# Four of six tiles of y transposed by VectorE blocks and DMAs in place of TensorE

## The chip, the cores and the metric

The kernel runs on one core of a Trainium2 chip. The metric is the device time of one execution in microseconds. Before the change it is 945.48 us (median of 3 runs, 944.89 to 948.21).

## The reference, cut to what matters

Four batches of 448 tokens go through sigmoid attention (12 heads of 64), a gated two-layer stage and a token and channel mixer, all in float32.

```
x  = concat over heads of sigmoid(q k^T / 8 - log 448) v            # [448, 768]
xk = mu_k * x + (1 - mu_k) * x_prev ;  xr likewise                  # x_prev: the token before
y  = sigmoid(xr @ w_r) * (relu(xk @ w_k) ** 2 @ w_v)                # [448, 768]
h  = relu(y^T @ w_tok1) @ w_tok2                                    # mixes tokens: 448 -> 256 -> 448
u  = y + h^T
out = u + relu(u @ w_ch1) @ w_ch2                                   # mixes channels: 768 -> 1536 -> 768
```

## The kernel before

Activations lie with channels on the 128 partitions and tokens along the free axis, one batch at a time, in six tiles of 128 channels by 448 tokens. Every float32 operand of a product is carried as `hi + lo`, hi being the rounded operand and lo the remainder, and a product is three matmuls (hi·hi, hi·lo, lo·hi; lines 395, 397 and 398). `split` (lines 95 to 100) makes the pair: a copy on ScalarE or VectorE, then a subtraction on VectorE.

`first_part` computes one batch up to u. Its loop over six tiles at line 453 makes y: 24 matmuls per tile m against two chunks of w_v, then on line 459 VectorE multiplies the sum in PSUM into `rows[m]`. The token mixing that follows contracts over tokens, so it needs y with tokens on the partitions. `y_transpose(m)` (lines 442 to 451) does that on TensorE: four transposes of up to 128 by 128 into one PSUM buffer (line 448), then two splits out of PSUM into the tiles `yt` (tag A2), one for the first 384 tokens and one for the last 64, whose hi and lo share a chunk. It is called for tile m-1 in the middle of the product of tile m (line 458), and for the last tile after the first product of the token mixing (line 474). The token mixing (line 464) works on two halves of the channels: half 0 reads tiles 0 to 2 of `yt` in each of its matmuls, half 1 tiles 3 to 5.

Weights come as float64. On first use a chunk is loaded into a tile `raw` (pool `wraw`, two buffers), made float32 by `narrow` and stored to DRAM; later it is read back into `wd` (line 315, two buffers). `w_tick` (line 340) keeps this going: a split into `whi` and `wlo` (three buffers), then the next loads. All DMAs are issued by SyncE. The attention of the next batch is handed out between the products of the current one.

The order on each engine is made by the framework from tiles and dependences; the buffers of one tag are given out in the order of the code, while an instruction whose operands and buffer are there may stand ahead of code that comes before it.

Of the kernel before, what the change touches and what calls it, by code (L numbers as in the profile page):

```python
# [9 lines left out]
F32 = mybir.dt.float32  # L10
F32R = mybir.dt.float32r
U32 = mybir.dt.uint32
# [19 lines left out]
def f32(ap):  # L32
    return ap.bitcast(F32)
# [9 lines left out]
EARLY = 20  # L43
TOK2 = 20


# Heads (batch, head) whose second product runs in plain float32: more for TensorE, less for the
# engines that split operands.
NATIVE = {(0, 1), (0, 7), (0, 4), (1, 1), (0, 3), (1, 8), (1, 4), (0, 6), (0, 2), (0, 5), (1, 9), (0, 11)}


# [5 lines left out]
def kernel(  # L57
# [13 lines left out]
    w_ch2: bass.AP,  # L71
    out: bass.AP,
):
    # Activations lie channels by tokens, one batch at a time; lay_out() and kernel() make
    # and undo the layouts of the inputs and of the output.
    # Every float32 operand of a matrix product is carried as hi + lo, both float32r, where
    # hi is the rounded operand and lo the exact remainder.
    nc = tc.nc
    PE, ACT, DVE, POOL, SP = nc.tensor, nc.scalar, nc.vector, nc.gpsimd, nc.sync

# [14 lines left out]
    def split(hi, lo, src, engine):  # L95
        if engine is ACT:
            ACT.copy(hi, src)  # L97
        else:
            DVE.tensor_copy(hi, src)
        DVE.tensor_tensor(out=lo, in0=src, in1=f32(hi), op=ALU.subtract)  # L100

    # ---------------------------------------------------------------- attention
    # Keys and values of a head: three chunks of 128 tokens, and the last 64 tokens twice, so
    # that hi and lo of what multiplies them share one contraction.
    kns, qns, vns = {}, {}, {}

    def load_k(g):
# [11 lines left out]
            vns[g] = a2.tile([P, 2, 4, D], F32, tag="vn", name="vn")  # L119
            SP.dma_start(out=vns[g], in_=v[g])  # L120

    # The table that holds every function in use is loaded while the first inputs come.
    warm = const.tile([P, 1], F32, tag="warm", name="warm")
    DVE.memset(warm, 0.0)
    ACT.activation(warm, warm, AF.Sigmoid)
    # TensorE comes up to its clock on zeros meanwhile.
    zero = const.tile([P, S], BF16, tag="zero", name="zero")
    POOL.memset(zero, 0.0)
    idle = ps_av.tile([P, 512], F32, tag="av", name="idle")
# [20 lines left out]
        DVE.tensor_scalar(out=om, in0=m, scalar1=-1.0, scalar2=1.0, op0=ALU.mult, op1=ALU.add)  # L150
        mus[name] = (m, om)

    # x of one batch from column 1 on; column 0 is what precedes the first token.
    xe = big.tile([P, NT, 1 + S], F32, tag="xe", name="xe")
    POOL.memset(xe[:, :, 0:1], 0.0)

# [81 lines left out]
        DVE.tensor_tensor(out=xe[me, pr, 1:], in0=ps[me, :S], in1=tmp[me], op=ALU.add)  # L238

    def attention_units(b, then=()):  # L240
        # then: for each pair of heads what follows its part of x
        u = [lambda: unit_k(b, 0, 0), lambda: unit_q(b, 0, 0), lambda: unit_k(b, 0, 1)]
        for pr in range(NPAIR):
            nx = pr + 1 < NPAIR
            u.append(lambda pr=pr: unit_qk(b, pr, 0, 0))
            u.append(lambda pr=pr: unit_q(b, pr, 1))
            if pr:
                u.append(lambda pr=pr: unit_av(b, pr - 1, 1))
                u += [f[pr - 1] for f in then]
            u.append(lambda pr=pr: unit_qk(b, pr, 0, 1))  # L250
            if nx:
                u.append(lambda pr=pr: unit_k(b, pr + 1, 0))
            u.append(lambda pr=pr: unit_qk(b, pr, 1, 0))
            u.append(lambda pr=pr: unit_av(b, pr, 0))
            if nx:
                u.append(lambda pr=pr: unit_q(b, pr + 1, 0))
                u.append(lambda pr=pr: unit_k(b, pr + 1, 1))
            u.append(lambda pr=pr: unit_qk(b, pr, 1, 1))
        u.append(lambda: unit_av(b, NPAIR - 1, 1))
        u += [f[NPAIR - 1] for f in then]  # L260
        return u

    # ---------------------------------------------------------------- weights
    # They come in float64. Each chunk is made float32 when it is first used, kept so in
    # DRAM, and read from there afterwards.
    def narrow(dst, raw):
        # dst, uint32 words: the float32 of the float64 whose two words lie in raw.
        # The scale takes the exponent's bias from float64's to float32's; of the low word
        # the top three bits are left, rounded so that they stay three.
        lo, hi = raw[..., 0], raw[..., 1]  # L270
        ACT.activation(f32(dst), f32(hi), AF.Copy, scale=2.0**-112)
        if ENG("low", 0) is ACT:
            ACT.activation(lo, lo, AF.Copy, bias=0.4375, scale=0.875 * 2.0**-29)
        else:
            DVE.tensor_scalar(out=lo, in0=lo, scalar1=0.875 * 2.0**-29, scalar2=0.4375, op0=ALU.mult, op1=ALU.add)
        DVE.scalar_tensor_tensor(  # L276
            out=dst, in0=dst, scalar=3, in1=lo, op0=ALU.logical_shift_left, op1=ALU.bitwise_or
        )
        DVE.scalar_tensor_tensor(  # L279
            out=dst, in0=hi, scalar=0x80000000, in1=dst, op0=ALU.bitwise_and, op1=ALU.bitwise_or  # L280
        )
# [73 lines left out]
        wst["due"] = i  # L355
        return splits.pop(i)

    # w_tok2 stays on chip.
    wt2h = const.tile([P, 2, S], F32R, tag="wt2h", name="wt2h")
    wt2l = const.tile([P, 2, S], F32R, tag="wt2l", name="wt2l")  # L360

# [5 lines left out]
            narrow(d.bitcast(U32), raw)  # L367
            split(wt2h[:, j], wt2l[:, j], d, DVE)

    # ---------------------------------------------------------------- mixing  # L370
    def pair_tiles(tag, n):
        return tuple(big.tile([P, n], F32R, tag=tag + s, name=tag + s) for s in "hl")

# [13 lines left out]
        )  # L387
        split(col(dst[0], t), col(dst[1], t), t2, ENG("mix", b))

    # ---------------------------------------------------------------- moe and mixer  # L390
    def products(ps, n, count, parts, stacked=None):
        # parts yields per contraction tile: stationary hi, lo, moving hi, lo;
        # of the tile `stacked` the moving hi holds both.
        for i, (wh, wl, xh, xl) in enumerate(parts):
            PE.matmul(ps[:, :n], wh, xh, start=(i == 0), stop=False)  # L395
            if i != stacked:
                PE.matmul(ps[:, :n], wh, xl, start=False, stop=False)  # L397
            PE.matmul(ps[:, :n], wl, xh, start=False, stop=(i == count - 1))  # L398
            if i % 2 == 1 or i == count - 1:
                yield (3 if i % 2 == 0 else 6) * (n / 2.4 + 2.5)  # L400
                w_tick()
# [12 lines left out]
    def first_part(b, xr, xk, rows, u):  # L414
        rows[:] = [big.tile([P, S], F32, tag="r%d" % m, name="r%d" % m) for m in range(NT)]

        # r = sigmoid(xr @ w_r)
        for m in range(NT):
            ps = new_mm()
            yield from products(ps, S, NT, chunked(1, NT, xr))  # L420
            ACT.activation(rows[m], ps[:, :S], AF.Sigmoid)

        # kk = relu(xk @ w_k) ** 2
        kk = pair_tiles("M", 12 * S)
        for m in range(F // P):
            ps = new_mm()
# [7 lines left out]
                DVE.tensor_tensor(out=t2, in0=t1, in1=t1, op=ALU.mult)  # L434
            split(col(kk[0], m), col(kk[1], m), t2, ENG("kk", b))

        # y = r * (kk @ w_v); its transpose feeds the token mixing
        # (tokens in chunks of 128; of the last 64, hi and lo share a chunk).
        yt = pair_tiles("A2", 4 * C)
        ytv = [t.rearrange("p (r c) -> p r c", r=4) for t in yt]  # L440

        def y_transpose(m):
            ps = new_mm()
            psv = ps.rearrange("p (r c) -> p r c", r=4)
            ms = slice(m * P, (m + 1) * P)
            for r in range(4):
                n = P if r < 3 else TAIL
                PE.transpose(psv[:n, r], rows[m][:, r * P : r * P + n], ident)  # L448
            hi, lo = (t[:, :, ms] for t in ytv)
            split(hi[:, :3], lo[:, :3], psv[:, :3], ACT)  # L450
            split(hi[:TAIL, 3], hi[TAIL:, 3], psv[:TAIL, 3], ACT)

        for m in range(NT):
            ps = new_mm()
            for i, cost in enumerate(products(ps, S, 8, chunked(2, 4, kk))):
                yield cost
                if i == 1 and m:
                    y_transpose(m - 1)
            DVE.tensor_tensor(out=rows[m], in0=rows[m], in1=ps[:, :S], op=ALU.mult)

        # token mixing
        h1v = [t[:, : 2 * C].rearrange("p (j c) -> p j c", j=2) for t in pair_tiles("M", 12 * S)]
        wt1 = []
        for half in range(2):
# [35 lines left out]
                split(col(u[0][0], m), col(u[0][1], m), t1, ACT)  # L500
                split(col(u[1][0], m), col(u[1][1], m), rows[m], ACT)

    # Channel mixing takes two batches at a time, and the hidden channels in two halves.
    # Of the earlier batch, the sum waits in DRAM.
    away = [dram.tile([P, S], F32, tag="u%d" % m, name="u%d" % m) for m in range(NT)]
    part = [dram.tile([P, S], F32, tag="p%d" % m, name="p%d" % m) for m in range(NT)]

# [26 lines left out]
                    elif i == 0:  # L534
                        SP.dma_start(out=part[m], in_=z)

    # ---------------------------------------------------------------- schedule
    def mix_units(name, box, b):
        def mix(t):
            if t == 0:  # L540
# [12 lines left out]
            w_ready(1)  # L553
    w_ready(2)

    # Attention and mixing of later batches go between the products of earlier ones.
    t_a = 432 * PASS + 44 * (HC / 2.4 + 2.5)
    t_c = 864 * PASS

# [34 lines left out]


def lay_out(x):
    """The inputs in the order in which the chip reads them; each value stays as it is."""
    import numpy as np

    def chunks(w, parts=1):  # L600
        # [K, N] -> per 128 columns and part of K: partition, tile of K, column
        kt = w.shape[0] // (P * parts)
        w = w.reshape(parts, kt, P, w.shape[1] // P, P).transpose(3, 0, 2, 1, 4)
        return w.reshape(-1, P, kt * P)
# [18 lines left out]
        "moe2_w_ch2": chunks(x["moe2_w_ch2"], 2),  # L623
    }
    y = {n: np.ascontiguousarray(a) for n, a in y.items()}
    # The chip has no float64: those arrays go as the 64-bit words that they are.
    return {n: a.view(np.int64) if a.dtype == np.float64 else a for n, a in y.items()}


# [39 lines left out]
```

## Time and profile before

| | us |
|---|---|
| median of 3 runs | 945.48 |
| profiled execution, first to last instruction | 939.8 |
| TensorE busy | 929.6 |
| VectorE busy | 658.3 |
| ScalarE busy | 517.4 |

The profile is one execution. Its span leaves out what lies before the first and after the last instruction, 5.7 us against the median. A busy TensorE is not one at its peak, as matmuls overlap; the chain of waits and the distance between starts tell what one costs. Idle time of an engine that isn't the bottleneck costs nothing.

### The profile page before, as it was taken

To read this page: it belongs to the slowest core of one execution; us is meant where nothing else is said; L and a number is where in the kernel's file an instruction comes from. 1 tells how busy PE (TensorE), PEld (TensorE's weight loads), DVE (VectorE), ACT (ScalarE), POOL (GpSimd) and SP (SyncE) were. 2 spreads that over 40 slices of the span, in tenths; PEclk is the share of its full clock that TensorE was granted. 3 is DMA by queue.
4 is the path that set the end of the run, shared out by engine and by line. 5 is a ranking of instruction groups with operands and counts; after the bars stand their busy time and mean duration, and the time that the engine had idled before them with its cause. 6 is when DMAs were issued, how large, how long until landed. Compare 5 with 4: busy or idle time off the path is not lost.

```text
span 939.8 us, 12086 instructions
## 1 busy us (share of the span) xinstructions
PE 929.6 (99%) x4472; PEld 816.0 (87%) x4472; DVE 658.3 (70%) x1087; ACT 517.4 (55%) x794; POOL 1.2 (0%) x8
## 2 busy tenths in 40 slices
PE   8999999999999999999999999999999999999998
PEld 4476778788999999999999999999999999999997
DVE  8999999988557997778779479988744463332231
ACT  6998988774664857546641367767444342112210
POOL 0000000000000000000000000000000000000000
PEclk9999999999999999999999999999999999999999
DMA  7636675674343466554535333323334331332131
GB/s 239 220 135 233 246 243 190 226 237 145 117 127 111 141 217 229 190 201 172 185 130 181 122 114 108 110 68 104 107 96 129 107 110 51 94 122 70 51 112 59
DMA packets 57082, 137.37 MB, mean 146 GB/s; under 512 B 6592, under 2 KB 23488, under 8 KB 57024
## 3 DMA queue, kind: packets, MB, share of 16 engines
q1 hardware_dynamic: 57024, 136.61, 43.6%
q8 instruction: 35, 0.57, 0.2%
q14 instruction: 23, 0.19, 0.1%
HBM read 106.96 MB, written 29.62 MB: 145 GB/s over the span
## 4 chain that ended last, share of the span: by engine, by line
PE 87%; DVE 7%; ACT 4%; DMA 2%; issue 1%; ACTq 0%; DVEq 0%
PE psmm L398 25%; PE psmm L395 25%; PE psmm L397 24%; PE psc L195 3%; PE psc L196 3%; PE pav L233 2%; PE pav L228 2%; PE pav L235 2%; PE psmm L448 1%; ACT a L202 1%; DVE wlo L100 1%; DVE wd L276 1%; DMA raw<-in_moe_w_k_dram 1%; DVE wd L279 1%; DMA raw<-in_moe_w_r_dram 1%
## 5 line engine op out<-in xcount | busy, mean ns | idle before, releaser
L97 ACT CAST whi<-wd 128x768 fp32r<-128x768 f32 (+1 forms) x160 | 121.4, 759 | 237.7 <-PE psmm L397 217.2
L100 DVE TENSOR_TENSOR wlo<-wd,whi 128x768 fp32r<-128x768 f32 (+1 forms) x160 | 137.6, 861 | 101.4 <-ACT whi L97 100.0
L395 PE MATMUL psmm<-Mh,whi 128*128 128x448 f32 x480 | 177.2, 369 | 0.1
L398 PE MATMUL psmm<-Mh,wlo 128*128 128x448 f32 x480 | 176.2, 367 | 0.1
L397 PE MATMUL psmm<-Ml,whi 128*128 128x448 f32 x480 | 175.5, 366 | 0.0
L395 PE MATMUL psmm<-A2h,whi 128*128 128x448 f32 (+1 forms) x400 | 145.2, 363 | 1.1 <-ACT whi L97 1.1
L398 PE MATMUL psmm<-A2h,wlo 128*128 128x448 f32 (+1 forms) x400 | 144.9, 362 | 0.8 <-DVE wlo L100 0.8
L397 PE MATMUL psmm<-A2l,whi 128*128 128x448 f32 (+1 forms) x384 | 139.2, 363 | 0.0
L397 PE MATMUL psmm<-A1l,whi 128*128 128x448 f32 x288 | 105.5, 366 | 0.1
L398 PE MATMUL psmm<-A1h,wlo 128*128 128x448 f32 x288 | 105.4, 366 | 0.0
L395 PE MATMUL psmm<-A1h,whi 128*128 128x448 f32 x288 | 105.2, 367 | 0.0
L202 ACT ACTIVATE a<-psc 128x896 f32<-128x896 f32 x96 | 86.9, 913 | 30.7 <-PE psc L196 30.2
L398 PEld LDWEIGHTS psmm<-Mh,wlo 128*128 128x128 f32 x480 | 90.2, 188 | 10.5 <-DVE wlo L100 1.6
L395 PEld LDWEIGHTS psmm<-Mh,whi 128*128 128x128 f32 x480 | 90.2, 188 | 9.0 <-issue 0.7
L397 PEld LDWEIGHTS psmm<-Ml,whi 128*128 128x128 f32 x480 | 90.2, 188 | 7.0
L395 PEld LDWEIGHTS psmm<-A2h,whi 128*128 128x128 f32 x400 | 75.1, 188 | 8.6 <-ACT whi L97 1.7
L398 PEld LDWEIGHTS psmm<-A2h,wlo 128*128 128x128 f32 x400 | 75.1, 188 | 8.1 <-DVE wlo L100 1.9
L397 PEld LDWEIGHTS psmm<-A2l,whi 128*128 128x128 f32 x384 | 72.1, 188 | 5.9 <-DVE A2l L100 0.3
L195 PE MATMUL psc<-Q,KK 128*128 128x448 f32 x192 | 71.6, 374 | 0.5 <-ACT a L202 0.4
L196 PE MATMUL psc<-Q,KK 128*128 128x448 f32 x192 | 70.3, 367 | 0.7 <-DVE Q L100 0.7
L209 ACT CAST ah<-a 128x896 fp32r<-128x896 f32 x72 | 67.7, 943 | 1.1
L395 PEld LDWEIGHTS psmm<-A1h,whi 128*128 128x128 f32 x288 | 54.0, 188 | 6.8 <-issue 1.4
(87 smaller groups left out, 1329.3 us busy)
## 6 DMA issues: line engine op xcount, KB each, us to landing
wd<-w SPq DMA_DIRECT2D x66, 384.0 KB, 3.0
raw<-in_moe_w_ch_dram SPq DMA_DIRECT2D x24, 768.0 KB, 4.6
w<-wd SPq DMA_DIRECT2D x38, 384.0 KB, 2.6
qn<-in_q_dram SPq DMA_DIRECT2D x48, 224.0 KB, 2.8
wd<-w SPq DMA_DIRECT2D x42, 256.0 KB, 2.6
kn<-in_k_dram SPq DMA_DIRECT2D x24, 256.0 KB, 2.7
vn<-in_v_dram SPq DMA_DIRECT2D x24, 256.0 KB, 3.1
raw<-in_moe_w_k_dram SPq DMA_DIRECT2D x8, 768.0 KB, 5.0
```

The costliest lines, as they stand in the source:

```text
L97: ACT.copy(hi, src)
L100: DVE.tensor_tensor(out=lo, in0=src, in1=f32(hi), op=ALU.subtract)
L195: PE.matmul(ps[:, j, :S], K[:, c * P : (c + 1) * P], Q1, start=True, stop=False)
L196: PE.matmul(ps[:, j, :S], K[:, c * P : (c + 1) * P], Q2, start=False, stop=True)
L202: ACT.activation(a, ps[:, :, :S], AF.Sigmoid, bias=-math.log(S), scale=1.0 / math.sqrt(D))
L209: ACT.copy(ah, a)
L228: PE.matmul(ps[:D, :S], vs[:n, c], st[c // 2][:n, c % 2], start=(c == 0), stop=(c == 3))
L233: PE.matmul(ps[:, :S], vs[:, c], ah[:, c % 2], start=(c == 0), stop=(c == 3))
L235: PE.matmul(ps[:, :S], vs[:, c], al[:, c % 2], start=False, stop=False)
L395: PE.matmul(ps[:, :n], wh, xh, start=(i == 0), stop=False)
L397: PE.matmul(ps[:, :n], wh, xl, start=False, stop=False)
L398: PE.matmul(ps[:, :n], wl, xh, start=False, stop=(i == count - 1))
```

## The change

For batches 1 to 3, tiles 0 to 3 of y are no longer transposed on TensorE. `y_turn(m)` lets VectorE transpose `rows[m]` in blocks of 32 by 32 into a tile `turn`, which two neighbouring tiles share and which takes a buffer of the pool `wraw`. After the second tile of a pair, 16 DMAs (4 positions of the block among the tokens, 4 among the channels) carry its blocks to their tokens' partitions, into columns of the tiles of kk that nothing else uses (`spare`). Each moves 32 partitions by 4 (or 3) runs of 256 bytes. They are issued on SyncE four at a time after each step of the product. `y_split(m)` then splits `spare` into `yt` with the same two splits as before, in the products of tiles 4 and 5. Tiles 4 and 5, and all of batch 0, go as before. The other lines of the diff take out comments and write out a helper.

```diff
+TURNED = 4
+TURN = 1
+BLK = 32
...
+        turned = TURNED if b >= TURN else 0
+        spare = [f32(t[:, 8 * S : 8 * S + 8 * P]).rearrange("p (r s c) -> p r s c", r=4, s=4) for t in kk]
+        turn, carry = {}, []
+
+        def y_turn(m):
+            if m % 2 == 0:
+                t = wraw.tile([P, NT, P, 2], U32, tag="raw", name="turn").rearrange("p t n e -> p (t n e)")
+                turn[m // 2] = f32(t[:, : 2 * S]).rearrange("p (g c) -> p g c", g=S // BLK)
+            tv = turn[m // 2]
+            at = m % 2 * BLK
+            DVE.transpose(tv[:, :, at : at + BLK], rows[m].rearrange("p (g c) -> p g c", c=BLK))
+            if m % 2:
+                for d in range(4):
+                    for s in range(4):
+                        to = spare[m // 2][d * BLK : (d + 1) * BLK, : 4 if d < 2 else 3, s]
+                        carry.append((to, tv[s * BLK : (s + 1) * BLK, d::4]))
+
+        def y_split(m):
+            ms = slice(m * P, (m + 1) * P)
+            at = m % 2 * BLK
+            src = spare[m // 2][:, :, :, at : at + BLK]
...
+            hi, lo = (t[:, :, ms] for t in ytv)
+            split(blocks(hi[:, :3]), blocks(lo[:, :3]), src[:, :3], ACT)
+            split(blocks(hi[:TAIL, 3:]), blocks(hi[TAIL:, 3:]), src[:TAIL, 3:], ACT)
+
         for m in range(NT):
             ps = new_mm()
             for i, cost in enumerate(products(ps, S, 8, chunked(2, 4, kk))):
                 yield cost
                 if i == 1 and m:
-                    y_transpose(m - 1)
+                    (y_turn if m - 1 < turned else y_transpose)(m - 1)
+                for to, src in carry[:4]:
+                    SP.dma_start(out=to, in_=src)
+                del carry[:4]
+                if m >= 4 and i in (2, 3) and 2 * (m - 4) + i - 2 < turned:
+                    y_split(2 * (m - 4) + i - 2)
             DVE.tensor_tensor(out=rows[m], in0=rows[m], in1=ps[:, :S], op=ALU.mult)
```

## Rows read from the trace of the kernel before

**Rows 1.** The page: span, and each engine's busy us, share and instructions.
```profile
span 939.8 us, 12086 instructions
...
PE 929.6 (99%) x4472; PEld 816.0 (87%) x4472; DVE 658.3 (70%) x1087; ACT 517.4 (55%) x794; POOL 1.2 (0%) x8
```

**Rows 2.** All waits of TensorE from 211 us on: total us, times, longest.
```profile
PE pav L235 <- DVE al L215: 0.3, 1, 0.3
PE pav L233 <- DVE ah L216: 0.2, 1, 0.2
```

**Rows 3.** The chain that ended last, batch 3: start us, us, what.
```profile
736.99 0.44 PE psmm L448 x4
...
742.30 0.44 PE psmm L448 x4
```

**Rows 4.** Line 448: count, duration ns min/median/max, first and last start, forms.
```profile
L448 PE MATMUL psmm<-ident,r x96: 270/272/327, 149.4 to 747.3; 128*128 128x128 f32 x72, 128*64 128x128 f32 x24
```

**Rows 5.** Groups of VectorE by line: count, busy us, mean ns, idle before.
```profile
L459 DVE TENSOR_TENSOR r<-r,psmm 128x448 f32<-128x448 f32 x24 | 14.8, 618 | 7.0 <-PE psmm L398 6.8
...
L99 DVE CAST Q<-qn 128x448 fp32r<-128x448 f32 x36 | 14.0, 390 | 3.8 <-PE psc L195 3.2
```

**Rows 6.** SyncE's timeline at the program's start: start us, us, issue.
```profile
3.07 0.43 SPq L115 DMA_DIRECT2D qn<-in_q_dram  x1
3.54 0.43 SPq L120 DMA_DIRECT2D vn<-in_v_dram  x1
```

**Rows 7.** DMA issues: count, KB each, median us from issue to landing.
```profile
wd<-w SPq DMA_DIRECT2D x42, 256.0 KB, 2.6
...
u<-r SPq DMA_DIRECT2D x12, 224.0 KB, 2.0
```

**Rows 8.** SyncE's timeline, batch 3, products of tiles 4 and 5.
```profile
735.85 0.32 SPq L315 DMA_DIRECT2D wd<-w  x1
...
738.24 0.32 SPq L315 DMA_DIRECT2D wd<-w  x1
...
741.15 0.32 SPq L315 DMA_DIRECT2D wd<-w  x1
```

**Rows 9.** VectorE's timeline, batch 3, around the end of tile 3's product.
```profile
734.60 0.62 DVE L459 TENSOR_TENSOR r<-r,psmm 128x448 f32<-128x448 f32 x1 [0.61 <-PE psmm L398]
735.14 0.68 DVE L100 TENSOR_TENSOR wlo<-wd,whi 128x512 fp32r<-128x512 f32 x1
...
738.13 0.55 DVE L100 TENSOR_TENSOR A2l<-psmm,A2h 128x384 fp32r<-128x384 f32 x1
```

**Rows 10.** ScalarE's timeline, batch 3, tile 5's product.
```profile
739.75 0.62 ACT L97 CAST whi<-wd 128x512 fp32r<-128x512 f32 x1 [0.77 <-PE psmm L397]
...
742.77 0.48 ACT L97 CAST A2h<-psmm 128x384 fp32r<-128x384 f32 x1
```

**Rows 11.** TensorE's timeline: first matmul of the token mixing, batches 3, 1, 2.
```profile
745.01 0.34 PE L395 MATMUL psmm<-A2h,whi 128*128 128x384 f32 x1
...
309.09 0.34 PE L395 MATMUL psmm<-A2h,whi 128*128 128x384 f32 x1
...
638.31 0.34 PE L395 MATMUL psmm<-A2h,whi 128*128 128x384 f32 x1
```

**Rows 12.** VectorE's timeline: end of tile 3's product in batches 1 and 2.
```profile
296.37 0.62 DVE L459 TENSOR_TENSOR r<-r,psmm 128x448 f32<-128x448 f32 x1 [0.76 <-PE psmm L398]
...
624.50 0.61 DVE L459 TENSOR_TENSOR r<-r,psmm 128x448 f32<-128x448 f32 x1
```

**Rows 13.** Timelines of SyncE and VectorE: loads issued early, and their users.
```profile
189.58 0.35 SPq L306 DMA_DIRECT2D raw<-in_moe_w_ch_dram  x1
...
308.08 0.95 DVE L279 SCALAR_TENSOR_TENSOR wd<-raw,wd 128x768 uint32<-128x768 uint32 x1
...
272.73 0.42 SPq L499 DMA_DIRECT2D back<-u  x1
...
321.63 0.61 DVE L494 TENSOR_TENSOR r<-r,psmm 128x448 f32<-128x448 f32 x1
```

More of the change, by code (lines that the diff above doesn't have):

```diff
@@ L99, in split @@
             DVE.tensor_copy(hi, src)
-        DVE.tensor_tensor(out=lo, in0=src, in1=f32(hi), op=ALU.subtract)
+        DVE.tensor_tensor(out=lo, in0=src, in1=hi.bitcast(F32), op=ALU.subtract)
     kns, qns, vns = {}, {}, {}
@@ L451, in y_transpose, with blocks @@
             split(hi[:TAIL, 3], hi[TAIL:, 3], psv[:TAIL, 3], ACT)
+        turned = TURNED if b >= TURN else 0
[17 more added lines that the diff above has]
+            src = spare[m // 2][:, :, :, at : at + BLK]
+            def blocks(t):
+                return t.rearrange("p r (s c) -> p r s c", c=BLK)
+            hi, lo = (t[:, :, ms] for t in ytv)
+            split(blocks(hi[:, :3]), blocks(lo[:, :3]), src[:, :3], ACT)
+            split(blocks(hi[:TAIL, 3:]), blocks(hi[TAIL:, 3:]), src[:TAIL, 3:], ACT)
         for m in range(NT):
```

## The prediction, made before the changed kernel ran

> **What bounds the kernel now.** I read the page first: TensorE is busy 929.6 of 939.8 us, VectorE 658.3, ScalarE 517.4 [rows 1]. The reader should see one full engine and two with room. A busy TensorE need not be at its best, so next came the list of its waits: from 211 us to the end only two, 0.5 us together [rows 2]. All three batches that the change touches lie in that stretch, and the chain there is matmuls on end. So each nanosecond taken from TensorE's queue there comes off the time, and each that TensorE is made to wait goes on. Last came the timelines around the spot, for what TensorE would have to wait for.
>
> **What is removed.** In the chain the four transposes of a tile take 0.44 us [rows 3]; the duration of a single one (272 ns [rows 4]) overlaps the next and is not the price. The kernel has 96 transposes, 24 groups of four [rows 4]. The change takes away four groups in each of three batches: 12 x 0.44 = 5.3 us. That is the whole gain there can be, 0.56% of 945.48, hardly over the 0.5% (4.7 us) that a measurement of this kernel can tell from no change.
>
> **What is added, and where it lies.** Splits: the same 24 on ScalarE and VectorE with another source, counted as nothing, since both engines have room [rows 1]. VectorE: 12 transposes of 128x448, which the trace does not show. A cast of that shape takes 390 ns, a multiply 618 [rows 5]; below nothing is excluded, as it is new work. I take 0.62, as it is a rearranging pass and not the plain copy, and allow 0.39 to 1.24. Off TensorE's path these 7.4 us cost nothing, unless they are late.
>
> SyncE: 6 x 16 = 96 DMAs. Issues that follow one another start 0.47 us apart [rows 6]; the shortest spacing, 0.32 for an issue after a pause [rows 8] and the 0.04 between issues in rows 6, would be 0.36. So 16 carries hold the queue 7.5 us. Behind them wait weight loads and, in batches 1 and 2, loads of q, k and v. From issue to landing, the quickest kind of large transfer takes 2.0 us, a weight load 2.6 [rows 7]. A carry moves far less (24 or 32 KB) but in small runs, which no row shows; I take 1.9, a little below the quicker, and 1.5 to 2.6 as bounds.
>
> **The new wait.** Tiles 0 and 1 have two products' time to arrive, so they cost nothing. The second pair is late by nature: its carries can start only when tile 3 has been multiplied and turned, and half 0 of the token mixing reads tile 2 in its very first matmul. Before, only 0.44 us on TensorE and two splits lay between. I lay out the chain from T, the start of line 459 for tile 3: multiply 0.62, one other VectorE instruction in between (in batch 3 a weight split is due at that moment [rows 9]) 0.62, transpose 0.62: T+1.9. Fifteen spacings of 0.47 are 7.05, two weight loads fall in between (as in batch 3 [rows 8]), 0.94: last issue at T+9.9, landed at T+11.8. ScalarE's copy 0.48 [rows 10] and a handover, 0.1: hi at T+12.4. VectorE's subtraction 0.55 [rows 9]: lo at T+13.0, which the second matmul needs 0.17 after the first.
>
> TensorE gets there, by the first matmul of the token mixing [rows 11] less T [rows 9, 12] less 0.44 for the one group that goes in between, at T+10.0 in batch 3 (745.01 - 734.60 - 0.44), at T+12.3 in batch 1 (309.09 - 296.37 - 0.44) and at T+13.4 in batch 2 (638.31 - 624.50 - 0.44); in the latter two attention fills the products. So TensorE waits 13.0 - 10.0 - 0.17 = 2.8 us in batch 3, 0.5 in batch 1, none in batch 2. In batch 3 nothing can fill the wait: no later attention is left and all that follows needs the token mixing. Sum: -5.3 + 3.3 = -2.0. From the profiled span 939.8 that gives 937.8; the 5.7 us around it stay, so 943.5 by the median.
>
> **Ends of this case.** Quick: cast's price 0.39, no instruction between, spacing 0.36, landing 1.9: lo at T + 0.62 + 0.39 + 5.4 + 0.72 + 1.9 + 0.58 + 0.55 = T+10.2, no wait in any batch: -5.3, 940.2. (A landing of 1.5 adds nothing to that.) Slow: transpose 1.24, two instructions between, landing 2.6: lo at T+15.0, and one more VectorE instruction ahead of the subtraction 15.7: waits of 5.5, 3.2 and 2.1, together 10.8: +5.5, 951.0.
>
> **What the order of the queue does.** The code issues four carries per step, between weight loads. That needn't be the order run. A raw chunk is loaded at 189.58 that VectorE finishes at 308.08, and a load of line 499 is issued at 272.73 while the sum that the code places before it, on line 494, first runs in that batch at 321.63 [rows 13]. So loads go as soon as buffer and operand are there, and carries will likewise. By the order of the code the last four come after about as many loads, so the sum hardly changes. Of the pool `wraw`, two buffers, the pair's tile takes one: in batch 1 the early raw loads [rows 13] must wait until the carries have read it. They are used only in the channel mixing, some 20 us on, so I cost that at nothing.
>
> The Trainium skill (DMA: Bandwidth & Descriptors, "Rules for kernel authors") speaks against this change: many small transfers should be joined, as under 64 KB one pays mostly overhead. Its fit (section "Anatomy of one DMA", for another issuing path) of 2.0 us plus size over 436 GB/s gives an estimate of 2.1 us a carry in place of 1.9, so 0.2 later in two batches: 943.9. Rows 6 show issues going on each 0.47 us, so this fixed part is paid once per burst, not 16 times.
>
> **Rivals.**
> 1. All is hidden (the quick end): 940.2. For it: a lone issue takes 0.32, and carries are small. Against it: issues in a row have never run quicker than 0.47 in rows 6. It needs the burst in under 6.5 us.
> 2. Weight loads held up behind the carries: slower. Place: SyncE's queue. A weight chunk loaded at 735.85 lands 2.6 later at 738.45, and its split (0.62 + 0.68 [rows 9, 10]) must be over when the token mixing uses it at 745.01: 5.2 us of slack. A burst without break holds a load 7.5 us, 2.3 too long, in six bursts: +13.8 on the sum, 957. It decides once a load waits over 5.2 us, that is for over 11 carries, or when a carry's issue takes over 0.33 us more than a load's: 0.8 each, with two runs per partition to lay out, would do it for even seven. Against it: loads come first in the code, so a ready load should overtake.
> 3. ScalarE stands waiting: its copies of `y_split` are in order with weight splits and sigmoids; if they are put before carries land, the split of the first token mixing weights goes behind four copies (1.5 us) and its subtraction, about 2.5 us more in batches 1 and 2, 1 in batch 3: +6, 949.5. For it: the copy of line 97 at 739.75 is due 5 us before tile 2 can be there [rows 10]. Against it: that copy is ready earlier, so it should go first.
> 4. The change does not do what it says: TensorE gets back the transposes' time only as idle time, all in the wait for tile 2, no change: 945.5. That is the middle of the first case's range, not a separate one.
>
> **How the numbers follow.** The main case, with the wait in batch 3 and a part in batch 1: 0.57; it spreads over 940.8 to 950.2 nearly whole, so nearly all counts as same. Rival 1: 0.14, all of it faster. Rival 3: 0.14, half of it over 950.2. Rival 2: 0.13, slower. What of the main case goes past either bound is small: I put 0.02 to faster and 0.06 to slower. Faster 0.16, same 0.58, slower 0.26. The range reaches down to the quick end, 940, and up past rival 3 and the slow end, to 952; outside it lie rival 2 and little else.
>
> **What would show it.** Right: 48 rows of line 448 instead of 96; 12 VectorE transposes of 0.4 to 1.2 us; 96 new issues on SyncE 0.36 to 0.47 us apart; a new wait of TensorE of some 2 to 3 us at the first matmuls of batch 3's token mixing, released by the split of `spare`, a shorter one in batch 1, and hardly another. Wrong: issues nearer 1 us; waits of TensorE for weight splits in the products of tiles 2 to 5 (rival 2); ScalarE idle before a copy out of `spare` with weight splits behind it (rival 3); no wait at all (rival 1). The forecast also falls if the new order of the queues moves attention elsewhere, which no row here can show.

## The result and the profile after

The changed kernel takes 959.53 us (median of 4 runs, 953.87 to 961.34), the kernel before in the same comparison 946.85 (944.89 to 948.51): 1.3% slower, ratio 1.0126, 95% interval 1.0096 to 1.0157. The forecast was 943.5, between 940 and 952. The kernel before itself scattered from 940.4 to 953.3 in the comparisons that followed; one reason is told below.

The page after, its span and busy times, which answers to [rows 1]:

```profile
span 957.8 us, 12194 instructions
...
PE 935.5 (98%) x4424; PEld 813.0 (85%) x4424; DVE 666.1 (70%) x1099; ACT 516.5 (54%) x794; POOL 1.2 (0%) x8
```

48 matmuls fewer and 12 VectorE instructions more, as the diff says. TensorE is busy 5.9 us longer in spite of that and waits 12 us more. Its waits over the whole execution, longest total first (us in total, times, longest), answering to [rows 2]:

```profile
PE psmm L399 <- ACT A2h L101: 6.5, 1, 6.5
PE psmm L399 <- ACT whi L101: 4.9, 3, 2.2
PE psc L199 <- ACT a L206: 1.6, 4, 0.6
```

The first is the wait for tile 2 at batch 3's token mixing, from 754.7 to 761.16. Of the second, 2.2 us stand in batch 3 at 746.9, in the product of tile 5; the rest is in batch 0. Of the third, 0.4 us stand at the start, the rest among attention's matmuls ahead of the token mixing of batches 1 and 2. (Lines have moved by 4 to 40: 395 is now 399, 97 is 101, 459 is 499; the carries are line 495.)

What the queue did meanwhile, SyncE's timeline in batch 3 (start, us, issues; neighbours of one kind in one row):

```profile
733.29 0.32 SPq L319 DMA_DIRECT2D wd<-w  x1
733.89 5.64 SPq L495 DMA_DIRECT2D Mh<-turn  x8
739.63 0.54 SPq L319 DMA_DIRECT2D wd<-w  x1
740.21 5.08 SPq L495 DMA_DIRECT2D Mh<-turn  x8
745.40 1.01 SPq L319 DMA_DIRECT2D wd<-w  x2
746.50 1.89 SPq L495 DMA_DIRECT2D Ml<-turn  x3
749.80 0.33 SPq L319 DMA_DIRECT2D wd<-w  x1
750.17 3.17 SPq L495 DMA_DIRECT2D Ml<-turn  x5
753.44 0.53 SPq L319 DMA_DIRECT2D wd<-w  x1
754.01 5.08 SPq L495 DMA_DIRECT2D Ml<-turn  x8
```

Eight carries in a row take 5.1 us (the first eight 5.6), 0.64 each, not 0.47. Tile 3 had been turned at 743.27, but the queue still held the first pair's carries and then weight loads; the second pair's begin at 746.50.

The load at 745.40 had its buffer free from 738.36 on, when VectorE's split at 737.67 was done (first line of VectorE's timeline below; before the change a load went 0.03 us after such an end [rows 8, 9]). It stood 7.0 us behind carries and one other load, and made the weight split late that TensorE waits for until 749.10. The same late split stopped the queue itself, from 748.39 to 749.80: the next load needs the buffer that this split frees, and thirteen carries of the second pair stood behind that load. The chain of waits that ends with the token mixing's matmuls, followed back from 765 us, runs through this place (start, us, what):

```profile
745.40 2.93 DMA wd<-w
...
748.43 0.63 ACT whi L101
749.08 0.70 DVE wlo L104
749.80 0.33 SPq L319
```

The chain landed as follows. VectorE's timeline in batch 3, then line 469 as a whole (duration min/median/max), then the carries (count, KB each, us to landing):

```profile
737.67 0.69 DVE L104 TENSOR_TENSOR wlo<-wd,whi 128x512 fp32r<-128x512 f32 x1
...
741.96 0.62 DVE L499 TENSOR_TENSOR r<-r,psmm 128x448 f32<-128x448 f32 x1 [3.05 <-PE psmm L402]
742.62 0.65 DVE L469 STREAM_TRANSPOSE turn<-r 128x448 f32<-128x448 f32 x1
```
```profile
L469 DVE STREAM_TRANSPOSE turn<-r x12: 635/639/646, 281.1 to 742.6; 128x448 f32<-128x448 f32 x12
```
```profile
Mh<-turn SPq DMA_DIRECT2D x24, 32.0 KB, 1.9
...
Mh<-turn SPq DMA_DIRECT2D x24, 24.0 KB, 1.9
```

The transpose was taken at 0.62 and took 0.64; the landing was taken at 1.9 and took 1.9.

The long wait has a second price. Stretches of batch 3 in windows (us; busy us and instructions of PE, PEld, DVE, ACT, POOL; granted clock; DMA share and GB/s):

```profile
720.00:740.00 20.00, 20.00 (x99) 18.16 (x98) 10.14 (x17) 5.37 (x9) 0.00 (x0) 1.00 0.47 137
...
758.30:765.10 6.80, 3.94 (x11) 3.56 (x12) 1.99 (x3) 1.76 (x3) 0.00 (x0) 0.50 0.41 129
```

TensorE was idle from 754.7; from 758.3 the granted clock is 0.50, the 1.2 GHz level, and it is back at 765.1. TensorE came back to work at 761.16, so it ran its first 3.9 us at half clock: 11 matmuls of 384 columns, which take 1.9 us at 0.17 each, took 3.9: 2 us lost.

### The profile page after: what moved, and what is told of

It reads as the page before. It is cut to its first block, busy times and chain, and to the rows that moved or that the text cites. A ratio compares the mean times of both kernels' runs of the same rounds, so it can differ in the third digit from the quotient of the medians.

```text
span 957.8 us, 12194 instructions
## 1 busy us (share of the span) xinstructions
PE 935.5 (98%) x4424; PEld 813.0 (85%) x4424; DVE 666.1 (70%) x1099; ACT 516.5 (54%) x794; POOL 1.2 (0%) x8
## 4 chain that ended last, share of the span: by engine, by line
PE 80%; DVE 8%; DMA 5%; ACT 3%; SPq 2%; issue 1%; DVEq 0%; ACTq 0%
PE psmm L399 24%; PE psmm L402 23%; PE psmm L401 23%; PE pav L237 2%; PE psc L199 2%; PE psc L200 2%; SPq L495 2%; PE pav L239 2%; DMA raw<-in_moe_w_r_dram 1%; PE pav L232 1%; DVE wlo L104 1%; DVE KK L104 1%; ACT a L206 1%; DMA raw<-in_moe_w_v_dram 1%; DVE wd L280 1%
```

## TensorE's pace, which moves the time of either kernel

The waits and the clock do not make up the 18.0 us between the two spans. The rest is in stretches without any wait. Between 345 and 600 us (channel mixing, attention, and from some 530 us on the first products of batch 2), in windows of 255 us: the kernel before, the same kernel profiled once more, the changed one, and that once more:

```profile
345.00:600.00 255.00, 255.00 (x1260) 236.36 (x1259) 198.17 (x314) 141.16 (x196) 0.00 (x0) 1.00 0.48 163
```
```profile
345.00:600.00 255.00, 255.00 (x1260) 236.36 (x1259) 198.08 (x314) 140.47 (x194) 0.00 (x0) 1.00 0.50 163
```
```profile
345.00:600.00 255.00, 255.00 (x1236) 231.62 (x1235) 195.55 (x307) 134.17 (x185) 0.00 (x0) 1.00 0.50 166
```
```profile
345.00:600.00 255.00, 255.00 (x1260) 236.41 (x1259) 199.18 (x315) 139.09 (x194) 0.00 (x0) 1.00 0.51 165
```

TensorE is full in all four and the granted clock is 1.00, but in the changed kernel's first profile it does 24 matmuls fewer. Taken from start to start in the timelines, the 448-column matmuls of an uninterrupted stretch lie either 202.7 or 206.5 ns apart on the mean, nearly the same from the stretch's first to its last. By this count (good to a few per cent) 2496 went at the slow pace in the changed kernel's first profile, 1446 in its second; in the kernel before 884 and 1464. These two runs, each a repeat of a known kernel, had been forecast as follows.

> The changed kernel once more, for TensorE's pace in long uninterrupted stretches. In its first profile 2496 matmuls went at 206.5 ns and 1416 at 202.7, in the kernel before 884 and 3037. Theory P1 (the pace is drawn anew in each execution): the stretch after batch 1, 1482 matmuls, can now be at 202.7, and the span then is 5.7 us shorter than 957.8, with the same waits of 6.5 and 2.2 us in batch 3. Theory P2 (the pace belongs to the program, set by the order of its instructions): the same stretches have the same pace.

Measured: 956.70 us, span 953.7. The stretch after batch 1 (1482 matmuls) now went at 202.7, the last one (868) at 206.65; the waits were alike, 5.0 us for tile 2 and 2.3 for the weight split. So P1.

> The kernel before once more, for TensorE's pace. If the pace of a long stretch is drawn anew in each execution, at least one of the long stretches (1343, 868, 329 and 327 matmuls; 202.7, 202.7, 206.4 and 206.5 ns in the first profile) has the other pace now, and the span moves by 0.0038 us for each matmul that changed, with no other wait of TensorE above 0.5 us after 211 us.

Measured: 945.98 us, span 943.9. The last stretch of 868 matmuls went at 206.64 where it had gone at 202.67, and a shorter one, of 327 matmuls before and 367 now, at 202.9 where it had been 206.5; no wait of TensorE above 0.2 us after 211 us. So the pace of such a stretch can differ from one execution to the next, with or without the change; 1600 matmuls more at the slow one are 6.2 us. Not every stretch varies: the one that begins at some 650 us went at 206.2 to 206.5 in all fourteen profiles. What sets the pace is not settled. The profiles show only that it changes where the stream of matmuls is interrupted, by transposes, by other shapes or by a wait.

For the change this means that a single pair of profiles misleads. The second ones have nearly the same number of slow matmuls, 1446 and 1464, and differ by 953.7 - 943.9 = 9.8 us. That is the better figure for the change's own cost in a profile; the 12.7 us of the medians include what four runs each happened to draw. The traces account for most of the 9.8: -5.3 for the transposes, +9.7 of TensorE's idle time after 203 us (9.9 against 0.1), +3.9 at the low clock (26 matmuls that took 7.8 us in two stretches of 0.50; that half of it is lost is an estimate), -1.0 for less idle time in batch 0. That makes some 7.3; what the rest is stays open.

## Experiments

**Without carries, and with four.** First no carries: `y_split` reads `turn` itself.

```diff
-                        carry.append((to, tv[s * BLK : (s + 1) * BLK, d::4]))
+                        pass
...
-            src = spare[m // 2][:, :, :, at : at + BLK]
+            tv = turn[m // 2]
+            src = tv[:, :12].rearrange("p (r s) c -> p r s c", s=4)[:, :, :, at : at + BLK]
...
```

> The changed kernel without its 96 carries: VectorE transposes as before, but the splits of tiles 0 to 3 read the tile 'turn' itself, so y of these tiles is in the wrong order (this part of the computation is left out). Theory Q (the queue of carries on SyncE makes TensorE wait: 6.5 us for tile 2 and 2.2 us for a weight split in batch 3, 2.3 us in batches 1 and 2, and a low clock of 6.8 us after the longest wait): all of that goes, the 5.3 us of the transposes stay saved: 941 us where TensorE's pace in uninterrupted stretches is as in the kernel before. Theory P (most of the loss is TensorE's pace, 206.5 ns for each matmul in place of 202.7 over the 270 us after batch 1, and has nothing to do with the carries): the waits go, but the time stays at some 948 to 952 us with the slow pace in that stretch. Theory V (the VectorE transposes themselves delay others): waits of TensorE for VectorE in batches 1 and 2, 946 or more.

Measured: 940.30 us (10 runs) against 944.42, ratio 0.9951, interval 0.9918 to 0.9983. TensorE's waits after 205 us are 1.4 us in all, the longest 0.7. So most of the gain is there when the carries are not (4.1 us between the medians), and no wait from VectorE's transposes is large (not theory V).

Then four carries a pair, each of one run of 1024 bytes on 128 partitions, with the data in the wrong place.

```diff
-                for d in range(4):
-                    for s in range(4):
-                        to = spare[m // 2][d * BLK : (d + 1) * BLK, : 4 if d < 2 else 3, s]
-                        carry.append((to, tv[s * BLK : (s + 1) * BLK, d::4]))
+                to = spare[m // 2].rearrange("p r s c -> p r (s c)")
+                for r in range(4):
+                    g = min(4 * r, 10)
+                    carry.append((to[:, r], tv[:, g : g + 4].rearrange("p g c -> p (g c)")))
```

> 4 DMAs a pair in place of 16, each moving one run of 1024 bytes on each of 128 partitions from SBUF to SBUF (y of tiles 0 to 3 goes to the wrong places). Tells what makes an issue 0.60 us: with runs of 1024 bytes it is 0.43 if small runs are the cause, 0.60 if it is that both ends are SBUF. No wait at the token mixing in either case; 937 to 943 us by the pace.

Measured: 940.41 us in a single run, no wait at the token mixing. SyncE's timeline in batch 3:

```profile
735.10 0.32 SPq L319 DMA_DIRECT2D wd<-w  x1
735.69 2.40 SPq L495 DMA_DIRECT2D Ml<-turn  x4
738.19 0.54 SPq L319 DMA_DIRECT2D wd<-w  x1
```

The four issues start 0.53, 0.64 and 0.64 apart: the first takes 0.47, each of the others 0.59 to 0.60, though each moves 128 KB in long runs. So small runs are not why an issue in a row is dear.

**One run on each of 128 partitions**, sixteen a pair.

```diff
-                for d in range(4):
-                    for s in range(4):
-                        to = spare[m // 2][d * BLK : (d + 1) * BLK, : 4 if d < 2 else 3, s]
-                        carry.append((to, tv[s * BLK : (s + 1) * BLK, d::4]))
+                for g in range(S // BLK):
+                    carry.append((spare[m // 2][:, g // 4, g % 4], tv[:, g]))
+                for g in range(2):
+                    carry.append((spare[m // 2][:, 3, 2 + g], tv[:, g]))
```

> 16 carries a pair as before, but each moves one run of 256 bytes on each of 128 partitions, where they moved 4 (or 3) runs on each of 32 (y of tiles 0 to 3 goes to the wrong places; the bytes are about the same). If the second level of the pattern makes an issue 0.60 us, it is now 0.43 to 0.47, the two bursts of a batch take 15 us in place of 20.6, and TensorE waits 3 us or less for tile 2 in batch 3: 946 to 949 us. If an issue takes 0.60 us whatever the pattern, because source and destination are both SBUF, the wait stays at 6 us and the time at 955 to 960.

Measured: 954.49 us (4 runs), ratio 1.0102, interval 1.0043 to 1.0161. In a row the issues take 0.60 us and start 0.64 apart, as before (only one that follows a load or a pause mostly takes 0.46 to 0.47, where with 32 partitions it took 0.59 to 0.60). The wait for tile 2 in batch 3 is 2.0 us, not the 6 that were forecast for this reading; 1.6 us for the weight split stand beside it, and 1.6 more at the token mixing in batches 1 and 2 each. So the pattern does not set the price in a row either. What the dear issues share is that source and destination are both SBUF: where one end is DRAM, issues in a row took 0.43 before [rows 6] and mostly 0.47 to 0.51 in the version over DRAM below. Why that should cost more no run shows.

**Half of the work.** Tiles 0 and 1 alone, or tiles 2 and 3 alone.

```diff
-TURNED = 4
+TURNED = 2
```

> Only tiles 0 and 1 are turned: one burst of 16 carries a batch, with two products of time behind it. Theory Q: no wait at the token mixing, no low clock; half of the gain, 2.7 us, is left: 944 us at the pace of before. Theory P: no wait either, but up to 7 us lost where the pace happens to be slow, up to 951. If weight loads behind one burst of 16 are enough to stop TensorE, a wait for the copy of line 101 of 1 to 2 us a batch is seen in the products of tiles 2 to 4.

Measured: 944.66 us (10 runs), ratio 1.0008, interval 0.9975 to 1.0040. No wait for tile 2, no low clock from 119 us on, but the 2.7 us do not show: in batch 3 TensorE waits 0.8 us for a weight split and 0.7 for its lower part, both behind the one burst, and in batch 2 it waits 1.2 us for VectorE's multiply.

```diff
-                    (y_turn if m - 1 < turned else y_transpose)(m - 1)
+                    (y_turn if 2 <= m - 1 < turned else y_transpose)(m - 1)
...
-                if m >= 4 and i in (2, 3) and 2 * (m - 4) + i - 2 < turned:
+                if m >= 4 and i in (2, 3) and 2 <= 2 * (m - 4) + i - 2 < turned:
```

> Only tiles 2 and 3 are turned and carried (by SyncE, as in the change); tiles 0 and 1 go through TensorE. Tells which burst makes the wait for tile 2. Theory Q1 (the burst of tiles 0 and 1 still fills the queue when tiles 2 and 3 are turned): without it the first late carry goes at T+2, and the chain of 16 issues 0.64 apart and two weight loads ends at T+12.7, landed T+14.6, copied T+15.2: the wait in batch 3 falls only by the 2.5 us that the queue was late, from 5.0 and 6.5 us (two profiles) to some 3.5 to 5, as 16 issues are too many by themselves. Theory Q2 (two bursts are too many, one would do): wait 1 us or less, no low clock. Time: -2.7 for the transposes, + wait and clock: 946 to 950 by Q1, 942 to 944 by Q2.

Measured: 951.92 us (4 runs), ratio 1.0101, interval 1.0071 to 1.0132. Here the late burst is alone. VectorE's, SyncE's and TensorE's timelines in batch 3:

```profile
741.50 0.62 DVE L499 TENSOR_TENSOR r<-r,psmm 128x448 f32<-128x448 f32 x1 [1.25 <-PE psmm L402]
742.04 0.68 DVE L104 TENSOR_TENSOR wlo<-wd,whi 128x512 fp32r<-128x512 f32 x1
742.64 0.64 DVE L469 STREAM_TRANSPOSE turn<-r 128x448 f32<-128x448 f32 x1
```
```profile
743.34 5.11 SPq L495 DMA_DIRECT2D Ml<-turn  x8
748.54 0.53 SPq L319 DMA_DIRECT2D wd<-w  x1
749.12 5.09 SPq L495 DMA_DIRECT2D Ml<-turn  x8
```
```profile
756.23 0.69 PE L399 MATMUL psmm<-A2h,whi 128*128 128x384 f32 x1 [4.56 <-ACT A2h L101]
```

With T at 741.50, the first carry goes at T+1.8 (forecast T+1.9, with the very instruction in between that had been assumed), the last at 753.61, T+12.1 (forecast T+9.9), with one load in between. TensorE waits 4.6 us for tile 2, then has a low clock of 6.8 us. So Q1: sixteen issues are too many by themselves.

**Other queues.** All carries on GpSimd's queue, or every second one.

```diff
-                    SP.dma_start(out=to, in_=src)
+                    POOL.dma_start(out=to, in_=src)
```

> All 96 carries are issued by GpSimd (0.55 us each, 0.58 apart, as measured with two queues); SyncE is as before the change. This tells the two ways apart in which the queue cost time. Weight loads are on time again, so no wait of TensorE for a weight split in batch 3. The carries still stand in one row of 32 in a batch, 18.6 us; in batch 3 the last one lands at about T+11.3 and a wait of 2 us for tile 2 stays. 941 to 944 us. If the long wait for tile 2 came from weight loads mixed into the carries alone, no wait stays at all: 939.

Measured: 948.10 us (10 runs), ratio 1.0017, interval 0.9980 to 1.0054. GpSimd's timeline, then TensorE at batch 3's token mixing:

```profile
725.00 9.24 POOL L495 DMA_DIRECT2D Mh<-turn  x16 [89.78 <-PE psmm L402]
734.83 9.24 POOL L495 DMA_DIRECT2D Ml<-turn  x16 [0.58 <-PE psmm L402]
```
```profile
745.98 0.69 PE L399 MATMUL psmm<-A2h,whi 128*128 128x384 f32 x1 [3.33 <-ACT A2h L101]
```

No wait for a weight split after batch 0 any more, since SyncE has only its own loads; but 16 issues of 0.58 still end too late, a wait of 3.3 us with 6.8 us of low clock behind it. The expectation had 2 us of wait and 941 to 944 us. The two ways are told apart: the weight split's 2.2 us come from sharing SyncE, and a wait of 3.3 us for tile 2 stays through the number of issues in one queue alone.

```diff
-                for to, src in carry[:4]:
-                    SP.dma_start(out=to, in_=src)
+                for n, (to, src) in enumerate(carry[:4]):
+                    (POOL if n % 2 else SP).dma_start(out=to, in_=src)
```

> Every second carry is issued by GpSimd's queue, which has nothing else to do; the rest by SyncE. Theory Q: SyncE is held half as long, the last carry lands about 6 us earlier in batch 3, and the wait for tile 2 is 0 to 1.5 us: 942 to 945 us at the pace of before, up to 951 at the slow one. If issues of GpSimd are much dearer than 0.64 us, its half becomes the late one and a wait of 3 us or more stays. If the DMA engines and not the issues bound the bursts, nothing changes: 955 to 960.

Measured: 939.46 us (10 runs) against 944.42, ratio 0.9954, interval 0.9923 to 0.9985. TensorE's waits after 205 us: 0.2 us. Nothing of what the change saves is waited away again.

> The version with carries on SyncE and GpSimd in turn once more, in five rounds, to see whether its lead over the kernel before holds: by its profile the 5.3 us of the transposes are saved and no wait above 0.3 us stands against them after 205 us, so 0.5% less than the kernel before, with both scattered by some 5 us either way through TensorE's pace. If the lead of 5 us in its first timing was the draw of paces, it is now within 0.2%.

Measured: 940.88 us (12 runs) against 942.74, ratio 0.9982, interval 0.9956 to 1.0008; again 0.2 us of waits. The two timings have leads of 5.0 and 1.9 us. The second is 0.18%, which by the expectation's own sign means that the first lead was in part a draw of paces. The profile had 1898 matmuls at the slow pace, the first one 970. Less 3.8 ns for each of these, the two spans are 933.4 and 932.1 us, those of the kernel before 938.3 and 936.4: on the mean 4.6 us less, an estimate near the removed 5.3. By its interval it is at most 0.1% slower than the kernel before; how much of the lead stays on the mean is not settled.

With two queues, batch 0 was given the change as well:

```diff
-TURN = 1
+TURN = 0
```

> The version with carries on SyncE and GpSimd in turn, for batch 0 as well: 16 more transposes off TensorE, 1.8 us, if batch 0's products (where weights are made float32 and loads of 512 to 768 KB fill the same queues) have room: 938 to 939, against 939.5 with batches 1 to 3. If the pool of raw weights, which the turned tiles now share while it is in use, holds weights back, TensorE waits in batch 0 between 150 and 205 us and it is 942 or slower.

Measured: 947.59 us (9 runs of 944.76 to 954.12; a tenth took 959.07), ratio 1.0060, interval 1.0032 to 1.0088. TensorE's waits before 205 us are 11.6 us, against 5.8 in the first run with two queues; 5.7 of them are for weight splits and their lower parts, against 2.8, the rest of the difference in attention. In batch 1 a wait of 1.4 us for the lower part of tile 2's split comes on top. That the shared raw buffers and not the queue hold the weights back was not told apart.

**Over DRAM.** Four writes put blocks in order, two reads bring them back.

```diff
-                for d in range(4):
-                    for s in range(4):
-                        to = spare[m // 2][d * BLK : (d + 1) * BLK, : 4 if d < 2 else 3, s]
-                        carry.append((to, tv[s * BLK : (s + 1) * BLK, d::4]))
+                held = dram.tile([S, 4, 2 * BLK], F32, tag="t%d" % (m // 2), name="held")
+                for s in range(4):
+                    SP.dma_start(out=held[:, s].rearrange("(g j) c -> j g c", j=BLK), in_=tv[s * BLK : (s + 1) * BLK])
+                to = spare[m // 2].rearrange("p r s c -> p r (s c)")
+                flat = held.rearrange("t s c -> t (s c)")
+                carry.append((to[:, :3], flat[: 3 * P].rearrange("(r p) c -> p r c", p=P)))
+                carry.append((to[:TAIL, 3], flat[3 * P :]))
```

> Instead of 16 carries from SBUF to SBUF a pair, four DMAs write the turned blocks to DRAM, where tokens and channels fall into order, and two read them back. Theory Q (what an issue costs times their number holds SyncE's queue): 6 issues of 0.43 us in place of 16 of 0.60; the second write-read trip adds some 2.5 us of landing. Chain in batch 3: turned at T+1.9, written by T+5.9, read by T+9.6, split by T+10.8: a wait of 0.5 to 1 us, none for weight splits; 939 to 942 us. If what made TensorE wait is the time in flight and not the queue, two trips in series are worse than the changed kernel's one: a wait of 3 us or more, 950.

Measured: 957.35 us (10 runs), ratio 1.0108, interval 1.0076 to 1.0140, a wait of 3.7 us for tile 2 in batch 3, as in the expectation's second reading. SyncE's timeline there, then DMAs (count, KB each, us to landing):

```profile
743.74 0.32 SPq L473 DMA_DIRECT2D held<-turn  x1
744.24 0.93 SPq L498 DMA_DIRECT2D Mh<-held  x2
745.27 1.00 SPq L319 DMA_DIRECT2D wd<-w  x2
746.32 1.51 SPq L473 DMA_DIRECT2D held<-turn  x3
751.30 1.05 SPq L319 DMA_DIRECT2D wd<-w  x2
752.53 0.91 SPq L498 DMA_DIRECT2D Ml<-held  x2
```
```profile
held<-turn SPq DMA_DIRECT2D x24, 112.0 KB, 3.0
...
Mh<-held SPq DMA_DIRECT2D x3, 384.0 KB, 3.5
Ml<-held SPq DMA_DIRECT2D x3, 384.0 KB, 4.9
```

The order in the queue costs time: one write of the second pair waits for VectorE until 743.74 with the first pair's reads behind it; the other three writes go only at 746.32, behind these reads and two loads; and from 747.8 to 751.3 a weight load waits with the second pair's reads behind it. But this last stop is worth under 1 us, as the reads had to wait for the writes in any case, and the last of them, issued at 747.31, landed at 751.65. Most of the rest is time in flight: two trips one after the other, 4.3 and 4.2 us for the second pair in batch 3, where a carry took 1.9. Fewer issues were no help here, as two landings had to follow each other.

## Why the prediction was wrong

**What bounds the kernel**, and that each nanosecond on TensorE counts: right. Without carries or with two queues most of the 5.3 us comes off. (The 5.7 us that the forecast put around the span are no constant. In the runs that have both on record, the time of an execution is 1.7 to 3.0 us above its own span; the rest of the 5.7 is that the profiled execution was a quick one. The sum does not suffer, as it goes from median to median.)

**The price of an issue: the step that failed.** I took 0.47 us from issues that read DRAM [rows 6] and put the dear end of the range there as well. From SBUF to SBUF it is 0.64. On 15 spacings that is 2.6 us in each chain. The slow end of the range had a dearer transpose, another instruction and a longer landing, but kept the spacing at 0.47; rival 2 named a dearer issue, but as 0.8 us.

**"Tiles 0 and 1 cost nothing": failed with it.** At 0.64, their sixteen carries and the loads between take 733.9 to 746.4 in batch 3, longer than the two products they were given. So the second chain began at T+4.5, not at T+1.9. These two terms move the last issue by 2.6 us each, and the queue's stop behind a waiting load (748.39 to 749.80) by 1.4 more: from T+9.9 to T+16.5 (758.5 - 741.96). TensorE itself came to the token mixing at T+12.7, not T+10.0; 2.2 us of the difference are the late weight split. So the wait for tile 2 is 6.5 us (5.0 in the second profile), not 2.8. The burst alone, in the run with tiles 2 and 3 only, gave 4.6.

**The other terms of that chain** were right: multiply 0.62, transpose 0.64 for 0.62, two loads in between, landing 1.9, the place of the wait, and that batches 1 and 2 hide theirs with attention. (The trace of before has large transfers that land in 1.9 too, so that 2.0 was not the quickest; the term stands. The instruction between multiply and transpose was not there in batch 3 of the changed kernel; in the run with tiles 2 and 3 alone it was.) In the changed kernel the waits at the token mixing of batches 1 and 2 are 1.4 and 1.0 us where 0.5 and 0 were forecast, but for attention's operands and not for tile 2: in batch 1, 20 of attention's score matmuls stand ahead of the first matmul of the token mixing (309.1 to 317.9 us), where there were none.

**Rival 2**, weight loads held up behind carries, came true beside the main case, once, in batch 3, and by its own rule: a load waited 7.0 us where 5.2 were free, and TensorE waited 2.2 us. It took eight carries in a row and the rest of the eight before, not "over 11", as each held the queue 0.64. The argument against it, that a ready load should overtake, did not hold. The late split also stopped the queue for the 1.4 us above. Its total (957) lay near the result by luck: it had 2.3 us in each of six bursts, and after five of them TensorE waited for no weight split. Rival 3 (ScalarE standing in front of weight splits) was not seen as a cost: with the carries on two queues the copies and the weight splits stand on ScalarE as before, and TensorE waits 0.2 us. Rival 1 is what two queues give.

**What was not thought of**: the low clock after a long wait, some 2 us in the first profile and 4 in the second, and the pace, which moved either kernel's profile by up to some 6 us (1600 matmuls at 3.8 ns). A range for one measurement of this kernel had to be wider than the terms of the change asked for.

The Trainium skill's rule that the prediction weighed (DMA: Bandwidth & Descriptors, "Rules for kernel authors": join small transfers) was right about this change, but not by the fixed part of a transfer's time, which is paid once per burst as forecast (landing 1.9 us each, overlapping; the page's fit gave 2.1); it came in through the issues.

## What to carry to other kernels

Price a row of small DMAs by the issuing queue first: count times spacing, with the spacing from issues of the same kind (in a row, an issue with both ends in SBUF took 0.60 us here and one with an end in DRAM 0.43 to 0.51, each with 0.04 behind it), and follow every burst until it ends, since an early burst without slack is late for the next. A DMA that had to wait held all that stood behind it in its queue (1.4 us here), so look for those too. Work taken from the full engine is kept only if what replaces it is over in time; here a second issuing queue was enough to end the new waits. And where two profiles of one program differ, compare stretches without waits before reading anything into the total.

## What the runs showed that was not expected

The pace of uninterrupted 448-column matmuls, 202.7 or 206.5 ns at the same granted clock of 1.00, kept for some 1500 matmuls in a row and, in most stretches, not the same in each execution (above).

An issue from SBUF to SBUF in a row of such takes SyncE 0.60 us and GpSimd 0.55, with runs of 256 or 1024 bytes, on 32 or 128 partitions alike; the first of a row takes SyncE 0.46 to 0.47 on 128 partitions. The price passes to what comes next: a weight load right behind a carry took 0.53 to 0.54 us, after a pause 0.32 (timeline above).

In batch 3, waits of TensorE of 3.3 to 6.5 us each went with 3.4 or 6.8 us at the 1.2 GHz level. So did one of 2.3 us in the changed kernel's second profile (3.4 us from 741.0), while waits of 2.0 and 2.2 in other profiles did not. In the run with all carries on GpSimd, TensorE's idle 3.3 us ended at 745.98, the low clock lasted from 745.3 to 752.1 (window as above), and 16 matmuls of 384 columns with 4 transposes of tile 5 took the 6.1 us from there on, where at full clock they take 3.2 (0.17 each and 0.44, an estimate):

```profile
745.30:752.10 6.80, 6.12 (x20) 5.69 (x21) 2.14 (x4) 1.89 (x4) 0.00 (x0) 0.50 0.22 58
```
